# Dilated q and k as rows of eight, masks made on chip, and batch 1's attention moved to the end of gate stage 0

## The chip, the cores and the metric

The kernel runs on one NeuronCore of a Trainium2 chip. The metric is device time in microseconds for one execution. Inputs are read from and the output is written to HBM within that time.

## The reference

Eight batches of eight heads, 576 positions, head size 64. Heads 0 to 3 attend to a plain causal window of 32 positions, heads 4 to 7 to a dilated one (every fourth position, 32 of them). The attention output, 4608 tokens of 512 features, goes through a GEGLU block.

```python
mask_plain = (rel >= 0) & (rel < 32)
mask_dil = (rel >= 0) & (rel < 32 * 4) & (rel % 4 == 0)
scores = q @ k.T / 8, masked by head, softmax          # per batch and head, 576 x 576
attn = softmax(scores) @ v                             # (8, 8, 576, 64)
x = attn.transpose(0, 2, 1, 3).reshape(4608, 512)
out = (gelu(x @ w_gate) * (x @ w_val)) @ w_out         # 512 -> 1536 -> 512
```

q, k, v and the weights are float32, as is the output. The kernel computes in float16 with float32 sums.

## The kernel before

**Tiling.** The block runs in nine stages, one for each chunk of 512 tokens. A stage has 12 gate blocks (`ffn1`: for each block of 128 of the 1536 hidden features, four matmuls with `w_gate` and four with `w_val` over the four k-chunks `xT[0..3]`, then `geglu`, Gelu on ScalarE and the product on VectorE into `u_all`) and then four output blocks of 128 tokens (`ffn2`: 12 matmuls with `w_out`, then `store`). Attention is cut into 32 pairs of heads, four for each batch (`n // 4` is the batch; pairs 0 and 1 of batch 0 are plain, 2 and 3 dilated), and each pair fills 576 columns of one `xT[g]`. The attention of batch c + 1 is computed within stage c, mostly between matmuls of `ffn2`, by hooks.

**One pair of heads.** `emit_s` makes the scores in four PSUM banks from `qT` and `kT` (features on partitions), and ScalarE takes the exponential into a tile `P`. The mask comes in one of two ways: with `pe_mask` TensorE first writes a bias (0 or -60000, `bias_p` or `bias_d`) into the banks by a matmul with the identity; otherwise VectorE multiplies `P` by 0 or 1 afterwards (`emit_mask`). `emit_pv` multiplies `P` with ones (the denominators, part "den") and with v (part "num"). VectorE turns the denominators into reciprocals by two 32 x 32 block transposes (`norm_r` and `recip`, tiles `dt`, `rc`, `rb`) and multiplies the numerators (`norm_x`) into `xT`.

**Dilated layout.** Position 4i + r is element i of class r. Keys and queries of each class are 144 long; the first 128 are one block, the last 16 the rest; `last_keys` copies the last 64 keys of each class into `kTr` for the rest. `quads` reads four consecutive positions as one row of 1 KB.

**Start.** SP and ScalarE queues load q and k of batch 0 as rows of six (plain heads, `first_p`, 96 partitions) and rows of four (dilated heads, `first_d` with 128 partitions and `first_r` with the last 16), all float32. Pool's queue loads the identities and both masks from constants in HBM. 16 matmuls on ones (`warm`) run on TensorE while the loads are under way. Engines cast to float16, TensorE transposes (`t_plain`, `t_dil`, `t_rest`; the last from float32), and copies bring the transposes from PSUM into `qTp` and `qTd`. Pool issues the weights by casting DMA, `load_w(0..2)` (a third of `w_gate` and of `w_val` each), after its casts of q.

**Order.** It is written out by hand (`manual_schedule`): each engine runs its instructions in the order of the program text, and waits on semaphores. PSUM has eight banks, and each use names its banks. The four pairs of batch 0 are done before stage 0. In stage 0, the transposes for batch 1 follow gate blocks 8 (`t_dil`, `t_rest`), 9, 10 (`t_plain`) and 11 (`t_dil`, `t_rest`), and its scores, denominators and numerators stand at hooks in the four output blocks, which run one after another on banks 0 and 1. From batch 2 on, q and k are transposed by DMA.

**DMA order.** `gated` lets one DMA wait for the landing of another: the loads of batch 1's plain q and k wait for the second third of `w_val`, v of batch 1 for the second third of `w_out`, and the loads of batch 2 for the last third.

**Gate block 0 and 1.** In stages 0 and 1 they run together (`ffn1_two`), k-chunk by k-chunk over four bank pairs, so that each k-chunk is used as soon as its `xT` is there.

The functions that the diff touches:

Of the kernel before, what the change touches and what calls it, by code (L numbers as in the profile page):

```python
# [15 lines left out]
WIN = 32  # L16
DIL = 4
USCALE = 32.0


def _np_masks():
    p = np.arange(128)[:, None]

    def band(n, off=0):
        rel = np.arange(n)[None, :] + off - p
        return (rel >= 0) & (rel < WIN)

    main_p, last_p, tail_p = band(160), band(128), band(64, 64)
    main_d = band(128)

    rel = 48 + np.arange(16)[None, :] - p % 64
    rest_d = [(rel >= 0) & (rel < WIN) & (p // 64 == m) for m in range(2)]
    mp = np.concatenate([main_p, main_p, main_p, last_p, tail_p], axis=1).astype(np.float16)
    md = np.concatenate([main_d, rest_d[0], main_d, rest_d[1]], axis=1).astype(np.float16)
    return mp, md
# [3 lines left out]
def kernel(  # L39
# [19 lines left out]
    R6 = S // 6  # L59
    NCH = NT // CH  # L60
# [10 lines left out]

    mp_np, md_np = _np_masks()
    mp_dram = nc.inline_tensor(mp_np, name="mask_plain")
    md_dram = nc.inline_tensor(md_np, name="mask_dil")
    id_dram = nc.inline_tensor(np.eye(P, dtype=np.float16), name="attn_identity")
    id32_dram = nc.inline_tensor(np.eye(16, dtype=np.float32), name="identity_f32")
# [13 lines left out]
    ident32 = const.tile([16, 16], F32, tag="ident32")  # L90
# [31 lines left out]
    first_d = [x32[t][:, 0 : HK * 4 * D] for t in range(2)]  # L122
    first_r = [x32[2 + t][0:16, 0 : HK * 4 * D] for t in range(2)]

    def load_w(i):
        cs = slice(i * CH, (i + 1) * CH)
        nc.gpsimd.dma_start(out=wg_t[i], in_=moe_w_gate[:, cs].rearrange("(kc p) n -> p kc n", p=P))
        return nc.gpsimd.dma_start(
            out=wv_t[i], in_=moe_w_val[:, cs].rearrange("(kc p) n -> p kc n", p=P)
        )  # L130
# [27 lines left out]

    def rows(src, b, kb):
        n = min(P, S - kb * P)  # L160
        return n, src[b, 0:HK, kb * P : kb * P + n, :].rearrange("h p d -> p h d")
# [14 lines left out]
    def v_plain(b, sv, eng):  # L176
        for kb in range(5):
            k0 = min(kb * P, S - P)
            gated(eng.dma_start(out=sv[:, kb], in_=v[b, 0:HK, k0 : k0 + P, :].rearrange("h p d -> p h d")))
# [23 lines left out]
    def load_qk_dil(b):  # L203
# [6 lines left out]
        return qd, rd  # L210

# [76 lines left out]
    def t_dil(b, hp, qd, q0, k0, engs):  # L288

        qtd_ = tiles["qT", b][1]  # L290
        for t, c0 in ((0, q0), (1, k0)):
            for hl in range(2):
                for m in range(2):
                    nc.tensor.transpose(
                        ps16f[:, c0 + (2 * hl + m) * P : c0 + (2 * hl + m + 1) * P],
                        qd[:, t, 2 * hp + hl, 2 * m : 2 * m + 2, :].rearrange("p r d -> p (r d)"),
                        ident,
                    )
        for t, c0 in ((0, q0), (1, k0)):
            copy(  # L300
                engs[t],
                qtd_[:, t, 2 * hp : 2 * hp + 2].rearrange("p h m i -> p (h m) i")[:, :, 0:P],
                ps16f[:, c0 : c0 + 512].rearrange("p (c i) -> p c i", i=P),
            )

    def t_rest(b, hp, rd, r0):

        qtd_ = tiles["qT", b][1]
        f32 = rd[0].dtype == F32
        pv = (psf if f32 else ps16f)[:, r0 : r0 + P]  # L310
        for t in range(2):
            for hl in range(2):
                for m in range(2):
                    c0 = (4 * t + 2 * hl + m) * 16
                    h0 = (2 * hp + hl) * 4 * D + 2 * m * D
                    nc.tensor.transpose(
                        pv[:, c0 : c0 + 16], rd[t][:, h0 : h0 + P], ident32 if f32 else ident[0:16, 0:16]
                    )
        nc.vector.tensor_copy(
            qtd_[:, :, 2 * hp : 2 * hp + 2].rearrange("p t h m i -> p t (h m) i")[:, :, :, P:NCL],  # L320
            pv.rearrange("p (t c i) -> p t c i", t=2, i=16),
        )

    def emit_s(n, b0, pe_mask=False):
# [5 lines left out]
        if n == NHP:  # L330
            last_keys(b, 0, HK)
# [174 lines left out]
    def norm_r(n, b0, wide=False, flip=False):  # L506
        dt = nrm.tile([P, 18, 32], F32, tag="dt", bufs=1)
# [5 lines left out]
        nc.vector.transpose(dst, den)  # L513
        recip(n, dt)
# [77 lines left out]
    def ffn2(c, tb, bank, hooks=None):  # L592
        for fc in range(NNB):
# [26 lines left out]
    nc.gpsimd.dma_start(ident, id_dram.ap())  # L620
    nc.gpsimd.dma_start(mask_p, mp_dram.ap())
    for t, src, eng in ((0, q, nc.sync), (1, k, nc.scalar)):
        eng.dma_start(out=fh(first_d[t]), in_=quads(src, 0, HK, 0, 4 * P))
        eng.dma_start(out=fh(first_r[t]), in_=quads(src, 0, HK, 4 * P, S))
    nc.gpsimd.dma_start(ident32, id32_dram.ap())
    nc.gpsimd.dma_start(mask_d, md_dram.ap())
    sv0 = new_v(0)
    v_plain(0, sv0, nc.sync)
    first_vd = ldp.tile([P, HK * 4 * D], F32, tag="st", name="st0")
    nc.scalar.dma_start(out=fh(first_vd), in_=quads(v, 0, HK, 0, 4 * P))  # L630
    q6 = ldp.tile([R6, 2, 6, HK, D], F16, tag="qp", name="qp0")
    qd0 = ldp.tile([P, 2, HK, 4, D], F16, tag="qd", name="qd0")
# [3 lines left out]

    def r4(t):
        return fh(t).rearrange("p h (r d) -> p h r d", r=4)

    warm(16, 7)  # L640
# [6 lines left out]
    nc.vector.tensor_scalar(bias_p, mask_p, 1.0, 60000.0, ALU.subtract, ALU.mult)  # L647
    for hp in range(2):
        t_plain(0, q6, hp, 2 * hp, ("act", "dve"))
    nc.gpsimd.tensor_scalar(bias_d, mask_d, 1.0, 60000.0, ALU.subtract, ALU.mult)  # L650
    for hp in range(2):
        copy("pool", qd0[:, 0, 2 * hp : 2 * hp + 2], r4(first_d[0])[:, 2 * hp : 2 * hp + 2])
    load_v_dil_rest(0)
    load_w(0)
    v_cast(0, sv0)
    copy("pool", tiles["v", 0][1], r4(first_vd))
    w1 = load_w(1)
    load_w(2)

    def den(n, b0, wide=False):  # L660
        emit_pv(n, b0, ("den",), wide)
        norm_r(n, b0, wide)
# [4 lines left out]

    emit_s(0, 4, pe_mask=True)
    emit_s(1, 0, pe_mask=True)
    for hp, eng in ((0, "dve"), (1, "act")):  # L670
        copy(eng, qd0[:, 1, 2 * hp : 2 * hp + 2], r4(first_d[1])[:, 2 * hp : 2 * hp + 2])
    den(0, 4, wide=True)
    for hp in range(2):
        t_dil(0, hp, qd0, 4096 + 1024 * hp, 4608 + 1024 * hp, ("act", "dve"))
    for hp in range(2):
        t_rest(0, hp, first_r, P * hp)
    last_keys(0, 0, HK)
    den(1, 4, wide=True)
    emit_s(2, 0, pe_mask=True)
    num(0, 4)  # L680
    den(2, 4, wide=True)
    emit_s(3, 0, pe_mask=True)
    num(1, 4)
    den(3, 4, wide=True)
    num(2, 0)
    num(3, 2)


    gate["dma"] = w1
# [5 lines left out]
    qd1, rd1 = load_qk_dil(1)  # L695
# [16 lines left out]
    scores = {0: range(4, 8), 1: range(8, 12), 2: range(12, 17), 3: range(17, 22), 4: range(22, 27), 5: range(27, 32)}  # L712
    values_b = {1: range(8, 12), 2: range(12, 16), 3: range(17, 20), 4: range(22, 24), 5: range(27, 28)}
    values_a = {3: {4: 16}, 4: {2: 20, 6: 21}, 5: {1: 24, 4: 25, 7: 26}, 6: {1: 28, 4: 29, 7: 30, 10: 31}}
    biased = (6, 7, 9)
# [13 lines left out]
    for c in range(NCH):  # L729
# [5 lines left out]
        if c < 2:  # L735
            pairs = ((2, 3), (0, 1))
        else:
            pairs = (ends, (mm0 + 1, mm0 + 2))
# [136 lines left out]
```

The softmax here doesn't subtract the row's maximum and nothing guards it: scores larger than these inputs give would overflow.

## Time and profile before

| | us |
|---|---|
| median of 7 runs (lowest, highest) | 357.06 (356.34, 357.92) |
| the profiled execution | 357.03 |
| its span, first to last instruction | 355.2 |
| TensorE busy | 340.0 |
| VectorE, ScalarE, Pool busy | 203.5, 146.7, 79.3 |
| first matmul of stage 0 starts | 25.19 |
| first output block of stage 0 starts | 50.04 |
| first matmul of stage 1 starts | 67.98 |

The profile is of one execution. Its engines are PE (TensorE; PEld is its weight load), DVE (VectorE), ACT (ScalarE), POOL (GpSimd) and SP (SyncE, which issues DMAs). A line of the timeline has the start, the length, the engine, the source line, the operation with what it writes and reads, a count where like instructions are merged, and in brackets the idle time before it with what ended that. DMA issues show as DMA_DIRECT2D on the engine that issues them, and their data land later. The mean granted clock of TensorE is 0.995.

### The profile page before, as it was taken

Reading aid. Unit: us, or ns where it says so; the run is one execution under the profiler, and the core shown is the slowest. Engines: PE = TensorE matmul, PEld = TensorE weight load, DVE = VectorE, ACT = ScalarE, POOL = GpSimd, SP = SyncE. Lnnn points to the kernel's source line nnn. Section 1 sums busy time; section 2 is a strip of 40 time slices with the busy share of each in tenths; the row PEclk is TensorE's granted clock in tenths of the full one; section 3 lists DMA queues with packets and bytes.
Section 4 is the critical chain, followed back from the end, with each engine's and each line's share of the span. In section 5 each row is a group of like instructions: output and inputs, shape, how many; then the busy total and the mean of one; then the engine's idle time right before and its main releaser. Section 6 shows DMA issues by size and latency. Waiting matters only on the chain.

```text
span 355.2 us, 5974 instructions
## 1 busy us (share of the span) xinstructions
PE 340.0 (96%) x2330; PEld 164.1 (46%) x2330; DVE 203.5 (57%) x313; ACT 146.7 (41%) x217; POOL 79.3 (22%) x110
## 2 busy tenths in 40 slices
PE   7879999999999999999999999999999999999995
PEld 2554454444454444444544454444454444444442
DVE  3585456743486348784778765985399423303420
ACT  1733355253553355535562447236733223323320
POOL 2580334550413074063005400240000000000000
PEclk9899999999999999999999999999999999999999
DMA  8999999999899899999149952792200020020002
GB/s 189 243 195 215 219 152 200 179 162 248 178 116 194 183 174 142 235 181 135 61 135 193 128 117 89 168 165 56 89 2 0 31 89 1 2 89 30 2 30 89
DMA packets 107292, 45.31 MB, mean 128 GB/s; under 512 B 83040, under 2 KB 102496, under 8 KB 107264
## 3 DMA queue, kind: packets, MB, share of 16 engines
q1 hardware_dynamic: 84272, 31.21, 40.7%
q0 software_dynamic: 21456, 12.01, 26.6%
q10 hardware_dynamic: 1536, 1.70, 2.1%
q8 instruction: 18, 0.29, 0.4%
q14 instruction: 10, 0.08, 0.1%
HBM read 40.13 MB, written 9.44 MB: 140 GB/s over the span
## 4 chain that ended last, share of the span: by engine, by line
PE 68%; DMA 12%; DVE 12%; issue 3%; POOL 2%; ACT 1%; ACTq 0%; SPq 0%; DVEq 0%; POOLq 0%
PE ps L562 40%; PE ps L596 21%; PE ps L455 4%; DMA xT<-in_k_dram 4%; DMA st<-in_k_dram 3%; DMA wv<-in_moe_w_val_dram 3%; DMA wo<-in_moe_w_out_dram 2%; DVE dt L483 2%; DVE u_all L585 2%; DVE xT L537 2%; DVE rb L522 2%; DVE dt L513 2%; DVE P L383 2%; DVE xT L493 1%; DMA sv<-in_v_dram 1%
## 5 line engine op out<-in xcount | busy, mean ns | idle before, releaser
L585 DVE SCALAR_TENSOR_TENSOR u_all<-g,ps 128x512 f16<-128x512 f16 x108 | 72.8, 684 | 76.6 <-PE ps L562 68.1
L562 PE MATMUL ps<-xT,wg 128*128 128x512 f16 x432 | 114.0, 379 | 1.0 <-DVE xT L537 0.4
L562 PE MATMUL ps<-xT,wv 128*128 128x512 f16 x432 | 113.8, 379 | 0.7 <-ACT osb L607 0.3
L584 ACT ACTIVATE g<-ps 128x512 f16<-128x512 f32 x108 | 63.8, 597 | 121.3 <-PE ps L562 121.2
L596 PE MATMUL ps<-wo,u_all 128*128 128x512 f16 x432 | 100.3, 380 | 0.0
L562 PEld LDWEIGHTS <-wv 128*128 128x128 f16 x432 | 42.2, 98 | 53.3 <-issue 2.9
L562 PEld LDWEIGHTS <-wg 128*128 128x128 f16 x432 | 41.1, 98 | 48.6 <-issue 1.6
L596 PEld LDWEIGHTS <-u_all 128*128 128x128 f16 x432 | 39.4, 98 | 45.3 <-issue 0.6
L607 ACT ACTIVATE osb<-ps 128x512 f32<-128x512 f32 x33 | 19.7, 598 | 38.1 <-PE ps L596 37.5
L199 POOL CAST qp<-st 128x2048 f16<-128x2048 f32 x6 | 11.4, 1896 | 96.7 <-DMA sv<-in_v_dram 54.7
L513 DVE STREAM_TRANSPOSE dt<-ps 128x576 f32<-128x576 f32 x23 | 17.9, 777 | 14.7 <-PE ps L455 14.6
L522 DVE STREAM_TRANSPOSE rb<-rc 128x576 f32<-128x576 f32 (+4 forms) x34 | 25.3, 743 | 1.2
L375 ACT ACTIVATE P<-ps 128x1152 f16<-128x1152 f32 x16 | 18.1, 1131 | 17.1 <-PE ps L373 17.0
L353 ACT ACTIVATE P<-ps 128x960 f16<-128x960 f32 x16 | 15.5, 970 | 12.2 <-PE ps L343 12.1
L537 DVE TENSOR_TENSOR xT<-ps,rb 128x576 f16<-128x576 f32 x16 | 17.9, 1129 | 0.3
L609 DVE TENSOR_SCALAR osb<-ps 128x512 f32<-128x512 f32 x3 | 2.1, 692 | 27.8 <-PE ps L596 27.8
L455 PE MATMUL ps<-P,ones 128*64 128x96 f16 (+5 forms) x174 | 11.5, 244 | 4.6 <-DVE P L383 2.2
L383 DVE TENSOR_TENSOR P<-P,mask_p 128x1344 f16<-128x1344 f16 x14 | 12.7, 912 | 5.0 <-ACT P L354 5.0
L383 DVE TENSOR_TENSOR P<-P,mask_d 128x1152 f16<-128x1152 f16 x11 | 8.3, 755 | 10.2 <-ACT P L375 10.2
L455 PEld LDWEIGHTS <-ones 128*64 128x64 f16 x174 | 7.4, 108 | 14.1 <-issue 11.2
L183 POOL CAST vp<-sv 128x1024 f16<-128x1024 f32 x8 | 9.0, 1127 | 13.0 <-DMA sv<-in_v_dram 13.0
L483 DVE STREAM_TRANSPOSE dt<-ps 64x576 f32<-64x576 f32 x14 | 10.9, 781 | 0.4
(83 smaller groups left out, 242.8 us busy)
## 6 DMA issues: line engine op xcount, KB each, us to landing
out_dram<-osb SPq DMA_DIRECT2D x36, 256.0 KB, 2.0
sv<-in_v_dram SPq DMA_DIRECT2D x40, 128.0 KB, 3.7
st<-in_q_dram SPq DMA_DIRECT2D x24, 128.0 KB, 3.6
st<-in_k_dram SPq DMA_DIRECT2D x24, 128.0 KB, 3.6
qd<-in_q_dram POOLq DMA_DIRECT2D x7, 256.0 KB, 5.2
qd<-in_k_dram POOLq DMA_DIRECT2D x7, 256.0 KB, 7.1
vd<-in_v_dram POOLq DMA_DIRECT2D x7, 256.0 KB, 6.6
wg<-in_moe_w_gate_dram POOLq DMA_DIRECT2D x3, 512.0 KB, 7.2
```

Of the source, the lines that this page charges most:

```text
L375: nc.scalar.activation(pt, ps[:, b0 : b0 + 4, 0:DW], AF.Exp, bias=0.0, scale=scale)
L383: nc.vector.tensor_tensor(pt, pt, mb, ALU.mult)
L455: nc.tensor.matmul(o, lhs, rhs, start=st, stop=True, skip_group_check=True)
L483: nc.vector.transpose(dt[64 * hl : 64 * hl + 64].rearrange("p b c -> p (b c)"), both_rows(1 - hl, b0, hl))
L513: nc.vector.transpose(dst, den)
L522: nc.vector.transpose(rb[:, 0 : 32 * nb].rearrange("p (b c) -> p b c", c=32), bass.AP(tensor=rc.tensor, offset=rc.offset, ap=[rc.ap[0], [1 ...
L537: nc.vector.tensor_tensor(dst.rearrange("p (i m s) -> p i m s", m=2, s=2), num, rb.rearrange("p (s m i) -> p i m s", s=2, m=2), ALU.mult,)
L562: nc.tensor.matmul(ps[:, bank, :], w[:, kc, ns], xT[kc][:, tok], start=first, stop=end)
L584: nc.scalar.activation(g, ps[:, banks[0], :], AF.Gelu)
L585: nc.vector.scalar_tensor_tensor(u_all[:, nb, :], g, USCALE, ps[:, banks[1], :], ALU.mult, ALU.mult)
L596: nc.tensor.matmul(ps[:, bank, :], u_all[:, fc, tb * P : (tb + 1) * P], wo_t[fc // 4][:, fc % 4, :], start=(fc == 0), stop=(fc == NNB - 1),)
L607: nc.scalar.activation(osb, ps[:, bank, :], AF.Copy, bias=0.0, scale=1.0 / USCALE)
```

## The change

- **Dilated q and k of batches 0 and 1** are read as rows of eight positions (`eights`, 72 partitions, 2 KB a row) by one casting DMA each from Pool's queue (`load_eights`). `t_dil` has 16 transposes of 72 rows for a pair of heads where it had 8 of 128 rows and `t_rest` had 8 of 16 rows; `t_rest`, the float32 rows, their casts and the float32 identity are gone.
- **Masks and identity** are made by Pool with memsets and affine selects (`identity`, `mask_plain`, `mask_dil`); their constants and four DMAs are gone. `bias_p` is made by VectorE right after its first memset in program order, `bias_d` by VectorE instead of Pool.
- **Weights.** The first `load_w` waits for the last tile of v (`gate_v`) of batch 0. v follows q on SP's queue without waits, and the dilated v moves from ScalarE's queue to SP's, behind v. The plain q and k of batch 1 now wait for the last third of `w_gate`.
- **Attention of batch 0** is reordered: scores of both plain pairs, dilated transposes, both plain denominators, scores of both dilated pairs, then the rest. The plain numerators are copied by ScalarE and multiplied by Pool (`num_split`). `last_keys` is shared by VectorE and Pool. `warm` has 30 matmuls instead of 16.
- **Batch 1.** Only the plain transposes stay within the gate blocks, after 10 and 11. Scores of pair 4, both dilated transposes and `last_keys` follow gate block 11. Output blocks 0 and 1 run side by side on banks 2 and 3 in thirds of four matmuls (`third`), with scores 5, 6 and 7 and denominators between. The Gelu table is loaded at the end of the stage. Stages 1 to 3 use the mirrored banks.

```diff
+    def identity():
+        nc.gpsimd.memset(ident, 1.0)
+        for sign in (1, -1):
+            nc.gpsimd.affine_select(out=ident, in_=ident, pattern=[[sign, P]], ...)
+    def band(t, step, off):
+        for sign, base in ((1, off), (-1, WIN - 1 - off)):
+            nc.gpsimd.affine_select(out=t, in_=t, ...)
+    def mask_plain():
+        nc.gpsimd.memset(mask_p, 1.0)
+        band(mask_p[:, 0:PB].rearrange("p (r c) -> p r c", c=PW), 0, 0)
+        band(mask_p[:, PB : PB + P].rearrange("p (r c) -> p r c", r=1), 0, 0)
+        band(mask_p[:, PB + P : PH].rearrange("p (r c) -> p r c", r=1), 0, 64)
+        nc.vector.tensor_scalar(bias_p, mask_p, 1.0, 60000.0, ALU.subtract, ALU.mult)
+    def mask_dil():
+        nc.gpsimd.memset(mask_d, 1.0)
+        by_class = mask_d.rearrange("p (m i) -> p m i", m=2)
+        band(by_class[:, :, 0:P], 0, 0)
+        band(by_class[:, :, P:NCL], 64, 48)
...
     def load_w(i):
...
+        gated(both[0])
...
+    def load_eights(b):
+        q8 = ldp.tile([R8, 2, HK, 8, D], F16, tag="qd", name=f"qd{b}")
+        for t, src in ((0, q), (1, k)):
+            tiles["last"] = nc.gpsimd.dma_start(
+                out=q8[:, t].rearrange("p h r d -> p h (r d)"), in_=eights(src, b, HK, H)
+            )
...
-    def t_dil(b, hp, qd, q0, k0, engs):
+    def t_dil(b, hp, q8, b0, engs):
...
+                for r in range(4):
+                    c0 = ((hl * 2 + r % 2) * 2 + r // 2) * R8
                     nc.tensor.transpose(
+                        ps16[:, b0 + t, c0 : c0 + R8],
+                        q8[:, t, 2 * hp + hl, 2 * r : 2 * r + 2, :].rearrange("p r d -> p (r d)"),
+                        ident[0:R8, 0:R8],
                     )
...
-    def t_rest(b, hp, rd, r0):
...
     for t, src, eng in ((0, q, nc.sync), (1, k, nc.scalar)):
         eng.dma_start(out=first_p[:, t], in_=sixes(src, 0))
-    nc.gpsimd.dma_start(ident, id_dram.ap())
-    nc.gpsimd.dma_start(mask_p, mp_dram.ap())
-    for t, src, eng in ((0, q, nc.sync), (1, k, nc.scalar)):
-        eng.dma_start(out=fh(first_d[t]), in_=quads(src, 0, HK, 0, 4 * P))
-        eng.dma_start(out=fh(first_r[t]), in_=quads(src, 0, HK, 4 * P, S))
-    nc.gpsimd.dma_start(ident32, id32_dram.ap())
-    nc.gpsimd.dma_start(mask_d, md_dram.ap())
+    qd0 = load_eights(0)
     sv0 = new_v(0)
-    v_plain(0, sv0, nc.sync)
+    load_v_dil_rest(0)
+    identity()
+    mask_plain()
+    mask_dil()
+    gate_v = v_plain(0, sv0, nc.sync)
...
-    nc.scalar.dma_start(out=fh(first_vd), in_=quads(v, 0, HK, 0, 4 * P))
+    nc.sync.dma_start(out=fh(first_vd), in_=quads(v, 0, HK, 0, 4 * P))
...
-    warm(16, 7)
+    warm(30, 7)
...
+    gate["dma"] = gate_v
     load_w(0)
     v_cast(0, sv0)
...
+    def num_split(n, b0):
+        emit_pv(n, b0, ("num",))
+        rb = tiles.pop(("rb", n))
+        nc.scalar.copy(first_n[n], psf[:, b0 * 512 : b0 * 512 + S])
+        nc.gpsimd.tensor_tensor(xT[n][:, 0:S], first_n[n], rb, ALU.mult)
...
     emit_s(0, 4, pe_mask=True)
     emit_s(1, 0, pe_mask=True)
...
+    t_dil(0, 0, qd0, 4, ("dve", "dve"))
+    t_dil(0, 1, qd0, 6, ("act", "act"))
+    last_keys(0, 0, 2)
+    last_keys(0, 2, HK, nc.gpsimd)
+    load_w(1)
+    copy("pool", tiles["v", 0][1], r4(first_vd))
+    wg2, _ = load_w(2)
+    dt0, dt1 = (den(n, -2 * n, t.rearrange("p (b c) -> p b c", c=32)) for n, t in enumerate(first_t))
+    recip(0, dt0)
+    recip(1, dt1)
+    emit_s(2, 4, pe_mask=True)
+    emit_s(3, 0, pe_mask=True)
+    den(2, 4)
+    num_split(0, 4)
+    num_split(1, 0)
+    emit_pv(2, 2, ("num",))
+    den(3, 4)
+    norm_x(2, 2)
+    num(3, 0)
...
-    gate["dma"] = w1
+    gate["dma"] = wg2
...
-    qd1, rd1 = load_qk_dil(1)
+    qd1 = load_eights(1)
...
+            s_of(4)
+            t_dil(1, 0, qd1, 2, ("dve", "dve"))
+            t_dil(1, 1, qd1, 0, ("dve", "dve"))
+            last_keys(1, 0, HK)
+            mask_next()
+            third(0)
+            s_of(5)
+            den(4, -2)
+            third(1)
+            mask_next()
+            s_of(6)
+            den(5, -2)
+            third(2)
+            s_of(7)
+            ffn2(c, 2, 2, {3: [lambda: den(6, -2)], 9: [lambda: num(4, 4)]})
+            store(c, 2, 2, "act")
+            ffn2(c, 3, 3, {0: [lambda: den(7, -2)], 4: [lambda: num(5, 6)]})
+            store(c, 3, 3, "act")
+            num(6, 0)
+            num(7, 4)
+            gelu_table()
```

## The prediction

> **What bounds the kernel now.** I read the page first, then the table of stages, then the timelines of TensorE and Pool at the start, then VectorE at the end of stage 0.
>
> ```profile
> PE 340.0 (96%) x2330; PEld 164.1 (46%) x2330; DVE 203.5 (57%) x313; ACT 146.7 (41%) x217; POOL 79.3 (22%) x110
> ...
> PE 68%; DMA 12%; DVE 12%; issue 3%; POOL 2%; ACT 1%; ACTq 0%; SPq 0%; DVEq 0%; POOLq 0%
> ```
>
> TensorE is the bound nearly everywhere, and of the chain only the 12% on DMA and 12% on VectorE can be had back. The table of stages (columns: span, then busy time and count for each engine, granted clock, DMA share, GB/s) says where:
>
> ```profile
> 8.00:25.20 17.20, 12.80 (x181) 8.68 (x181) 12.57 (x23) 10.15 (x14) 11.52 (x16) 0.90 1.22 223
> 25.20:29.70 4.50, 3.97 (x21) 1.57 (x18) 3.50 (x5) 0.78 (x2) 2.27 (x4) 1.00 1.24 206
> 29.70:49.20 19.50, 19.27 (x121) 9.53 (x120) 9.61 (x16) 7.86 (x14) 6.61 (x9) 1.00 1.08 194
> 49.20:68.00 18.80, 17.97 (x182) 8.95 (x181) 12.93 (x22) 8.53 (x12) 6.83 (x8) 1.00 1.17 196
> ```
>
> The change touches these 68 us alone. The wide matmuls come 0.216 us apart (four in 0.86), so what counts is when they begin, and how much else stands between them. TensorE at the first gate stage:
>
> ```profile
> 25.73 0.39 PE L562 MATMUL ps<-xT,wv 128*128 128x512 f16 x1
> ...
> 27.79 0.38 PE L562 MATMUL ps<-xT,wg 128*128 128x512 f16 x1 [0.37 <-DVE xT L537]
> ...
> 29.68 1.03 PE L562 MATMUL ps<-xT,wg 128*128 128x512 f16 x4
> ```
>
> The first value matmul waits for `wv` (landed 25.72), the third and fourth k-chunks for VectorE's normalisation. The opening 16 matmuls end at 29.68; I call that moment E. From E to stage 1 (67.98) it takes 38.30 us. Pool:
>
> ```profile
> 2.98 0.59 POOL L626 DMA_DIRECT2D mask_d<-mask_dil  x1
> 10.82 1.19 POOL L650 TENSOR_SCALAR bias_d<-mask_d 128x288 f16<-128x288 f16 x1 [7.26 <-DMA mask_d<-mask_dil]
> 13.59 1.18 POOL L264 CAST qd<-xT 128x512 f16<-128x512 f32 x2 [1.58 <-DMA xT<-in_q_dram]
> ...
> 16.79 0.77 POOL L128 DMA_DIRECT2D wv<-in_moe_w_val_dram  x1
> ```
>
> Pool idles from 3.57 to 10.82. In the built program a library reload for Pool stands just before that TENSOR_SCALAR; it has no row, and whatever it costs lies in this gap. After the change the same reload stands before the first affine select, with nothing to hide it.
>
> **Masks on chip.** Four mask and identity DMAs go. Pool gets 3 memsets and 12 affine selects; identity and `mask_p` take 8 selects over 1600 columns, `mask_d` 4 over 576. No row is an affine select. Nearest: Pool casts (512, 1024, 2048 columns: 0.62, 1.04, 1.90 us), so 0.19 us plus 0.83 ns a column. Memsets at that rate make 1.05 us, the 8 selects 8 x 0.19 + 1600 x 0.83 ns = 2.85: 3.9 us. The other end is the TENSOR_SCALAR above, 4.1 ns a column: 7.6 us. I take 3.9, since 1.19 us for 288 columns looks like a first call. Pool first issues four DMAs (0.77, 0.77, 0.65, 0.65 from 1.22): free at 4.1. `mask_p` is ready at M = 8.0 without a reload cost, 11.7 with slow selects, and 15.2 if the reload costs all of the 7.2 us gap (its bounds are 0 and 7.2; I take 0, as the gap ends with the landing of `mask_d`, which explains it alone). A gain from the operation itself is excluded: it only adds to Pool.
>
> The Trainium skill speaks against this step: its page "GPSIMD Engine Reference", section 2.1 "Instruction dispatch", says that the first call after a code load pays some 6 us that no profile row shows. No row here shows that cost or excludes it; with it M would be 14.0, and an estimate by my sum would end near 360.
>
> Who waits: VectorE. `bias_p` is its second instruction, ahead of the memsets and the casts of q (1.03 us), so these wait for M + 0.34. Transposes end at M + 1.9 (casts 1.03, last 12 transposes 0.52). On the other side the 30 warm-up matmuls: 16 took 6.47 us at 0.427 apart, the change of rate showing near 7.1 us; 14 more at 0.216 end at 10.9, and 24 transposes at 43 ns make 11.95. So M is covered up to 10.0; beyond that each us counts. In return TensorE stays warm: the clock stood at 0.50 from 12 to 14 us, and the mask matmuls took 1.32 us where the dilated ones later take 0.65.
>
> **Eights by cast DMA.** Casts of `qd0` (Pool 1.18, VectorE 0.89, ScalarE 0.62) and 16 f32 remainder transposes (2 x 0.67 us, with a 0.73 us wait) go. In bytes landed, 3.9 MB ahead of the weights become 3.1, as dilated q and k land in f16 and the masks go. Up to v it is 2.6 MB: from 2 us at the 223 GB/s of the second stretch 13.5. q8 and k8 stand before half of v, so they are in time for their transposes at 14.6. v has 256-byte rows; 12 to 14 us, when they ran, had 154 GB/s, so I take v at 15 to 16.5. vd moves to SP's queue behind v, and is needed at 21.
>
> **w gated by v.** Pool issues w0 when the last v tile lands. The same transfer from an empty queue is in the trace: `wo` 1 and 2, issued from 44.04 (DMA share 0.33), landed by 52.49, 8.45 us. So w0 is there at 23.5 to 25, where it was 25.7. Behind the gated issue on Pool stand the v casts (1.50 us), half of `last_keys`, w1, the vd cast, w2 and two multiplies; `last_keys` is wanted first, for scores 3 at 18.5, and done at about 18.6.
>
> **Attention of batch 0.** From 11.95: scores 0 (0.65 + 0.40), exps to 14.6 and 16.1 (1.45 each), dilated transposes and copies to 17.3, first `dt` at 16.6. From there VectorE is unbroken: four `dt` at 0.78, four reciprocal pairs at 1.07, two products at 1.1 = 9.6 us, so the last xT at 26.2, and its four matmuls end at 27.1. The products of pairs 0 and 1 leave VectorE: ScalarE copies the numerators (0.64 each) after the last exp, 20.8 to 22.1, and Pool multiplies (no such row; between a 576-column cast, 0.67, and twice VectorE's 0.73; I take 1.0) after issuing w2 at 22.6, so 23.6 and 24.6. With w0 at 23.5 to 25 the 16 matmuls (3.46) end at 27.1 to 28.5. I take E = 27.6, which is 2.1 earlier.
>
> **Rest of stage 0.** Of E to the end of gate block 11 (19.54 us), one pair of dilated transposes (1.23) and one plain set (0.51) leave. From there to stage 1 were 18.76, of which 1.0 stalls:
>
> ```profile
> 58.02 1.68 DVE L383 TENSOR_TENSOR P<-P,mask_p 128x1344 f16<-128x1344 f16 x1
> 60.26 0.78 DVE L513 STREAM_TRANSPOSE dt<-ps 128x576 f32<-128x576 f32 x1 [0.57 <-PE ps L455]
> ```
>
> (the late mask, 0.79 on TensorE, and 0.2 for `wo`). The new order: 18.76 - 1.0 - 0.82 (old dilated set) + 0.51 + 2 x 0.69 (16 transposes at 43 ns) = 18.83, plus new waits. Scores 4 need banks 6 and 7, still held by the last plain transposes: 0.75. `den` 4 waits for its mask behind four copies on VectorE (0.42 or 0.75 each by the two copy rows; I take 0.75), `kTr` 0.29 and the mask 0.86: 1.3. `den` 5: 0.25. Sum 21.1; with 17.8 before it 38.9 against 38.3: +0.6. The Gelu table, now loaded ahead, spares the 0.3 stall at 73.2: +0.3. With the stalls at 0.8 or 3.3 instead it is -1.2 to +1.3. The rows of batch 1 wait for wg2 where it was wv1, but with 0.8 MB less ahead they land by about 40 (41.67 before); w1, w2 and `wo` are issued at about the same time or earlier. Later stages mirror their banks: nothing.
>
> **Sum.** -2.1 + 0.3 = -1.8. The profiled execution took 357.03 us (span 355.2), the median of the runs is 357.06. Forecast 355.2. What this kernel's measurement can tell from no change is about 0.2%, or 0.7 us.
>
> **The rivals.**
> 1. *Slower: Pool is late with the masks.* For it: the reload that has no cover any more, and VectorE standing behind it. Against: a gap that the mask's landing explains. It decides from M = 11.9, where the 1.8 us are used up: a reload of 3.9 us with fast selects. At 7.2 us, M = 15.2, 5.2 late, and TensorE idle after the warm-up, so again half clock (about 1 us): E = 33.8, and the end +4.4: 361.4.
> 2. *The gate costs what it saves.* v's small rows share DMA with q8 and k8. At 17.5 for v, w0 is there at 25.95, E = 29.4 and the end at 357.1; if v lands at 18.67, as it did, 358.2. Against: its tiles are now all issued by 4 us, where SP used to wait for the rows of q and k until 14.2.
> 3. *No change: slow selects alone*, M = 11.7, 1.7 late: 356.9.
>
> **How the numbers follow.** Forecast case 0.52 (own range 353.3 to 356.2, the tail's ends with E at 27.1 or 27.6); rival 1 0.27, rival 2 0.11 (0.04 of it within the bound), rival 3 0.10. Faster by over 0.2%: 0.52; within: 0.14; slower: 0.34. The range goes from 353.3 (E = 27.1, tail -1.2) to 361.0, close to the full reload.
>
> **What would show it.** Right: Pool's last select of `mask_p` before 10, `bias_p` at once, transposes at 10.9, clock 1.00 from 11 to 14; E at 27 to 28.5; gate block 11 to stage 1 about 21 us with waits of `den` 4 on its mask. Wrong: a gap on Pool before the first select; casts of q after 11; a wait for `wv` beyond 25; waits of TensorE on `qd` or `wo` in stage 0.

## The result, and the profile after

The changed kernel takes 356.04 us (median of 19 runs, 355.25 to 356.88), the kernel before 357.55 (47 runs beside them). The ratio is 0.9957, 95% interval 0.9947 to 0.9967: faster by about 1.5 us, where 1.8 were forecast. (The forecast of 355.2 was counted from 357.06; from the 357.55 measured here it would be 355.75.) The profiled execution of the changed kernel took 355.55 us with a span of 353.8 (before: 357.03 and 355.2). One execution of the run e9 below, the profiled one, ran at a granted clock of 0.56 throughout and took 579.77 us; no median and no ratio below has it in.

The number came out; the sum behind it only in part, and most of this document is about that. First the table of stages of the changed kernel (columns as before: stretch, its length, busy time and count of PE, PEld, DVE, ACT, POOL, granted clock, DMA share, GB/s). The stretches end at the first gate matmul, at E (the end of the opening 16 gate matmuls), at the end of gate block 11 and at the start of stage 1:

```profile
8.00:23.99 15.99, 11.83 (x192) 8.07 (x191) 13.49 (x28) 11.13 (x15) 10.41 (x18) 1.00 1.09 181
23.99:27.93 3.94, 3.61 (x16) 1.54 (x16) 1.93 (x2) 0.45 (x1) 3.52 (x4) 1.00 1.25 207
27.93:46.87 18.94, 17.96 (x94) 8.36 (x93) 8.24 (x12) 7.25 (x13) 3.70 (x5) 1.00 0.93 179
46.87:67.43 20.56, 19.11 (x210) 10.17 (x208) 14.72 (x24) 9.25 (x12) 6.77 (x11) 1.00 1.11 181
```

E is at 27.93 instead of 29.68: 1.75 us gained. From E to stage 1 it takes 39.50 instead of 38.30: 1.20 lost. Stage 1 starts 0.55 earlier. It opens without the stall behind the table load, and the last store leaves VectorE at 350.82 instead of 351.61: 0.79 earlier. The other 0.6 us of the span lie behind that moment: about 3.0 us from there to the end of the span instead of 3.6. The last copy of a store, before and after:

```profile
350.92 0.69 DVE L609 TENSOR_SCALAR osb<-ps 128x512 f32<-128x512 f32 x1 [9.60 <-PE ps L596]
```

```profile
350.13 0.69 DVE L622 TENSOR_SCALAR osb<-ps 128x512 f32<-128x512 f32 x1 [9.60 <-PE ps L609]
```

TensorE in stage 0 of the changed kernel:

```profile
23.99 0.38 PE L575 MATMUL ps<-xT,wg 128*128 128x512 f16 x1 [1.64 <-POOL xT L676]
...
25.34 0.38 PE L575 MATMUL ps<-xT,wg 128*128 128x512 f16 x1 [0.33 <-POOL xT L676]
...
44.87 0.43 PE L305 MATMUL ps<-ident,qp 96*128 96x96 f16 x6 [0.98 <-POOL qp L292]
...
53.17 0.48 PE L463 MATMUL ps<-P,ones 128*64 128x512 f16 x6 [0.81 <-DVE P L391]
```

In what follows w0, w1 and w2 are the three thirds of the weights, each with a gate half (`wg`) and a value half (`wv`), and the rows of batch 1 are its plain q and k (`st`). The first gate matmul waits for Pool's product; the weights were there, but not by much (`wv` of w0 landed 7.7 us after its issue at 16.07, at about 23.8). At gate block 10 the transposes of batch 1 wait 0.98 us for Pool's cast of rows that have only just landed. The chain of waits (start, length, what) shows that both waits hang on Pool's queue:

```profile
5.40 9.61 DMA sv<-in_v_dram
...
16.83 1.08 POOL vp L203
...
20.03 0.98 POOL vd L292
21.01 11.30 DMA wg<-in_moe_w_gate_dram
...
32.74 11.20 DMA st<-in_k_dram
...
45.30 1.74 PE ps L575 x8
```

From the landing of v the chain goes down Pool's queue to the issue of w2, through w2's landing to the issue of batch 1's rows, and through their landing to TensorE at gate block 10. E is not on it.

### The profile page after: what moved, and what is told of

Read it like the earlier page. It is cut to its first block, busy times and chain, and to the rows that moved or that the text cites. A ratio compares the mean times of both kernels' runs of the same rounds, so it can differ in the third digit from the quotient of the medians.

```text
span 353.8 us, 5997 instructions
## 1 busy us (share of the span) xinstructions
PE 338.4 (96%) x2338; PEld 163.7 (46%) x2338; DVE 201.4 (57%) x307; ACT 147.8 (42%) x219; POOL 81.4 (23%) x121
## 4 chain that ended last, share of the span: by engine, by line
PE 71%; DVE 12%; DMA 9%; issue 3%; POOL 2%; SPq 1%; ACT 1%; DVEq 0%; POOLq 0%; ACTq 0%
PE ps L575 41%; PE ps L609 22%; PE ps L463 4%; DMA wg<-in_moe_w_gate_dram 3%; DMA st<-in_k_dram 3%; DMA sv<-in_v_dram 3%; DVE u_all L598 2%; DVE dt L491 2%; DVE xT L550 1%; DVE xT L501 1%; PE ps L381 1%; DVE rb L535 1%; DVE P L391 1%; DVE dt L524 1%; SPq L197 1%
## 5 line engine op out<-in xcount | busy, mean ns | idle before, releaser
L524 DVE STREAM_TRANSPOSE dt<-ps 128x576 f32<-128x576 f32 x21 | 16.3, 777 | 15.1 <-PE ps L463 15.1
L391 DVE TENSOR_TENSOR P<-P,mask_p 128x1344 f16<-128x1344 f16 x14 | 11.9, 856 | 2.6 <-ACT P L362 2.5
L491 DVE STREAM_TRANSPOSE dt<-ps 64x576 f32<-64x576 f32 x14 | 10.9, 781 | 0.4
```

The costliest lines, as they stand in the source:

```text
L391: nc.vector.tensor_tensor(pt, pt, mb, ALU.mult)
L491: nc.vector.transpose(dt[64 * hl : 64 * hl + 64].rearrange("p b c -> p (b c)"), both_rows(1 - hl, b0, hl))
```

## The experiments

All were timed beside the kernel before; times below are medians, to be held against 356.04 for the changed kernel, and the ratios are to the kernel before. The kernel before had medians of 357.13 to 357.59 beside them, so that runs of different rounds are compared more surely by their ratios. The theory after the reading above was: E is set by Pool's queue, counted from the landing of v, and the tail's loss by the release of batch 1's rows through w2. The rival: weights, VectorE or the masks' chain set E.

### e1_w2_late

```diff
-    load_w(1)
+    _, wv1 = load_w(1)
     copy("pool", tiles["v", 0][1], r4(first_vd))
-    wg2, _ = load_w(2)
...
     num_split(1, 0)
+    load_w(2)
...
-    gate["dma"] = wg2
+    gate["dma"] = wv1
```

> The third weight chunk (w2) is issued by Pool behind its two multiplies instead of ahead of them, and the rows of batch 1 are released by the second chunk's value half instead of w2's gate half. Theory: the moment E (end of the opening 16 gate matmuls, 27.93 in the changed kernel) is set by Pool's queue, counted from the landing of v. Then the multiplies start when ScalarE's copies are done (21.2 and 21.9), the first gate matmul comes at 22.6 to 23.2 and E falls to 26.8 to 27.3, where VectorE's last product (25.9) sets it; the 1.0 us wait for Pool's casts of batch 1 goes too. Together 1.2 to 2.0 us less than the changed kernel: 354.0 to 354.9. Rival: the first weights themselves set E (TensorE's weight load also stood waiting for wv until 23.99), then E stays at 27.7 to 27.9 and only the second part shows, 355.0; and w2, issued 3 us later, would show as a wait at gate block 8.

Measured: 354.75, ratio 0.9927 (0.9913 to 0.9942), 1.3 us less than the changed kernel. Pool's products start at 21.41 instead of 22.50, the first gate matmul comes at 22.87, and E at 27.12: the theory's place. What sets E now is not VectorE's last product, as the theory had it, but the first weights, as the rival had it, with a wait of 0.63 us for `wv`:

```profile
21.41 2.76 POOL L676 TENSOR_TENSOR xT<-xT,rb 128x576 f16<-128x576 f32 x2 [0.16 <-ACT xT L675]
...
23.87 0.39 PE L575 MATMUL ps<-xT,wv 128*128 128x512 f16 x1 [0.63 <-DMA wv<-in_moe_w_val_dram]
```

The wait at gate block 10 did not go: it is 0.86. The rows' last half was issued 2.3 us earlier than in the changed kernel (30.43), but took 12.6 us instead of 11.2, so that Pool's cast of it starts at 43.06, only 0.93 earlier. w2, issued at 24.13, was under way beside it; that the sharing is the cause is argued, not shown. The gain of 0.9 at stage 1 (66.56 instead of 67.43) is the rows' gain as much as E's.

### e2_st_w1

```diff
-    gate["dma"] = wg2
+    gate["dma"] = wv1
```

> Only the release of the rows of batch 1: the second chunk's value half instead of w2's gate half. Theory: of the 1.2 us by which E to stage 1 grew (38.30 to 39.50), 1.0 is TensorE's wait for Pool's cast of those rows at 44.87; they are issued at 32.74 because wg2 releases them. Released some 3 us earlier they land by 41, the wait goes, and the time falls by 0.8 to 1.0 us: 355.0 to 355.3. Rival: the DMA engines are full (1.1 busy share and more) and the rows share them with w2, so they land as late as before, or w2 lands late instead: no change, 356.0, or a wait at gate block 8.

Measured: 355.50, ratio 0.9940 (0.9917 to 0.9963). The cast of the late half starts at 41.99 instead of 43.99 and the wait is gone:

```profile
41.99 2.37 POOL L292 CAST qp<-st 96x768 f16<-96x768 f32 x3 [3.91 <-DMA st<-in_k_dram]
```

But the seven executions fall in two groups: three with a mean granted clock of 1.00 at 354.26 to 354.42, four with 0.993 to 0.995 at 355.50 to 356.20. The profiled one is of the second kind. Its stretches from 20 us on:

```profile
20.00:24.00 4.00, 1.93 (x48) 1.52 (x45) 3.86 (x8) 3.25 (x4) 4.00 (x5) 0.97 1.23 205
24.00:26.00 2.00, 1.86 (x5) 0.71 (x5) 2.00 (x3) 0.00 (x0) 2.00 (x3) 0.50 1.24 206
26.00:28.00 2.00, 2.00 (x8) 0.75 (x6) 0.09 (x1) 0.00 (x0) 1.66 (x3) 0.70 1.24 207
```

TensorE was busy for 1.93 of the 4 us before 24, with 1.62 idle at the end, and then ran at half clock for about 3 us: the first gate matmuls are 0.43 apart instead of 0.216, and E is 29.09. So the theory's 0.8 to 1.0 was too small where the clock held (1.7), and in the others, if they ran as the profiled one did, the half clock ate nearly all of it.

### e4_masks_dma

```diff
+    nc.gpsimd.dma_start(ident, id_dram.ap())
+    nc.gpsimd.dma_start(mask_p, mp_dram.ap())
     qd0 = load_eights(0)
...
-    identity()
-    mask_plain()
-    mask_dil()
+    nc.gpsimd.dma_start(mask_d, md_dram.ap())
+    nc.vector.tensor_scalar(bias_p, mask_p, 1.0, 60000.0, ALU.subtract, ALU.mult)
```

> The masks and the identity by DMA from inline tensors again, as in the kernel before; all else as in the changed kernel. Theory: the start is bound by the bytes ahead of v; 0.35 MB of masks at the 223 GB/s of the stretch from 8 to 24 us are 1.6 us, so v lands at 16.6 instead of 15.0, w0 and Pool's queue move with it, and E comes 1.0 to 1.6 us later: 357.0 to 357.6. Rival: v does not move, as the DMA engines have room, and the masks come sooner than from Pool (bias_p before 8.3, casts of q with it): no change or up to 0.5 us faster, 355.5 to 356.0.

Measured: 357.96, ratio 1.0014 (0.9998 to 1.0029): without masks on chip the rest of the change gains nothing against the kernel before. By the medians the step is worth 1.9 us, but only 1.5 of it lies within the span (its last store leaves VectorE at 352.31 instead of 350.82). The rest lies outside it: in each of the twelve executions the time is 2.2 us longer than the span, in the changed kernel 1.7. Why, no run tells. Two Pool lines and one of VectorE:

```profile
16.24 0.76 POOL L162 DMA_DIRECT2D wg<-in_moe_w_gate_dram  x1 [10.42 <-DMA sv<-in_v_dram]
...
19.71 0.40 POOL L281 COPY kTr<-qTd 128x256 f16<-128x256 f16 x1 [0.59 <-ACT qTd L312]
```

```profile
9.55 0.34 DVE L661 TENSOR_SCALAR bias_p<-mask_p 128x672 f16<-128x672 f16 x1 [8.15 <-DMA mask_p<-mask_plain]
```

v is there 0.94 later (16.24 instead of 15.30), less than the 1.6 of the expectation, which took 0.35 MB for masks that are 0.27 in the profile of before (and 223 GB/s, which is the rate of the kernel before). And the mask by DMA is later than Pool's own: `bias_p` starts at 9.55 instead of 8.31, the transposes at 12.39 instead of 11.26, the clock falls to 0.63 from 12 to 16 us, and `kTr` on Pool then waits for this chain, not for v. E is 29.53; the k half's wait ends at 46.35 instead of 44.87.

### e5_ones_late

```diff
-    for vp_, _, vt_, _ in vset:
-        ...
     for hp in range(2):
         for t in range(2):
             cast_six(("dve", "act")[t], q6, first_p, t, hp)
     for hp in range(2):
         t_plain(0, q6, hp, 2 * hp, ("act", "dve"))
+    for vp_, _, vt_, _ in vset:
+        ...
     nc.vector.tensor_scalar(bias_d, mask_d, ...)
```

> VectorE's six memsets of ones in the value tiles (1.9 us, which stood between bias_p and the casts of q) move behind the transposes' copies. Theory: E is set through Pool by the landing of v (15.0), not by the masks' chain: the transposes come 0.8 to 1.0 us earlier (10.3 instead of 11.26), scores, exps and the dt of pairs 0 and 1 with them, but E stays within 0.3 of 27.93 and the time within 0.3 of 356.0. Rival: the chain masks, casts, transposes, scores, exps, dt, products sets E; then E and the time fall by 0.8 to 1.0, to 355.1.

Measured: 355.98, ratio 0.9963 (0.9949 to 0.9976): no change, as the theory said, with the transposes at 10.02 instead of 11.26 and the first denominators on TensorE at 14.86 instead of 16.10. With the gate on v, this chain has slack. E itself is 30.08 in the profiled execution, not within 0.3 of 27.93: behind an idle 1.84 us thirteen of the sixteen opening matmuls ran at half clock, 0.43 apart. Yet stage 1 starts only 1.0 later than in the changed kernel (68.42), since TensorE then no longer waits at gate block 10. The profiled execution, at 356.50, is one of three with a clock of 0.989 or 0.990, which took 356.50 to 356.64; the other six took 355.47 to 356.11.

### e10_fill

```diff
     num(3, 0)
+    warm(7, 4)
```

> Seven warm-up matmuls more (1.5 us at 0.216 apart, into a bank that the first gate block overwrites) in the 1.64 us in which TensorE waits for Pool's first product; nothing else changes. Theory: after such an idle stretch the granted clock falls to 0.50 in some executions (in the runs so far the opening 16 matmuls came 0.43 apart behind waits of 1.62 and 1.84 us), which moves E by 1 to 2 us; but in the changed kernel E does not set the time as long as it lies before about 29, because TensorE then waits at 44.87 for Pool's cast of the rows of batch 1, which are released by wg2. So the mean granted clock of all executions is 0.998 or more, and the time stays within 0.3 of 356.0. Rival: E sets the time, and the changed kernel's executions at 0.993 to 0.995 pay for the clock: then 355.3.

Measured: 355.86, ratio 0.9953 (0.9937 to 0.9970), all eight executions at a clock of 0.998 or more. Of the changed kernel's 20 executions (the profiled one included) 13 had a clock of 0.993 to 0.995, and they took no longer (median 356.04, the others 355.95). So the changed kernel has half clock in most executions and its time shows nothing of it. E itself can be seen in the profiled ones alone (28.02 here); that it came later in the 13 is inferred from their clock. What sets the time is the landing of the rows of batch 1, for which TensorE waits here too:

```profile
45.04 0.43 PE L305 MATMUL ps<-ident,qp 96*128 96x96 f16 x6 [1.06 <-POOL qp L292]
```

### e3_no_gate

```diff
-    gate["dma"] = gate_v
     load_w(0)
```

> The first weights are no longer held back until the last tile of v has landed: Pool issues them at about 10 us; all else as in the changed kernel. Theory: 1.05 MB of weights (f16 as landed; 5 us at the 205 GB/s of the following stretch) share the DMA engines with v, so v lands 2 to 4 us after 15.0; Pool's casts and products move by that less the 1.5 us of the two issues, E comes 1 to 2.5 us later, of which 1.0 is covered by the wait for the rows of batch 1: 356.0 to 357.8. Rival: w0 sets E, v hardly moves: the same or up to 0.5 us faster, 355.5 to 356.0.

Measured: 354.17, ratio 0.9906 (0.9886 to 0.9927), 1.9 us less than the changed kernel. The theory, that v would pay, was wrong by sign; the rival had the sign and v, but a quarter of the size, and its reason (w0 sets E) is not the one that the trace shows. Pool's queue in the ungated kernel:

```profile
9.88 0.78 POOL L140 DMA_DIRECT2D wg<-in_moe_w_gate_dram  x1
10.65 0.82 POOL L140 DMA_DIRECT2D wv<-in_moe_w_val_dram  x1
15.13 1.04 POOL L203 CAST vp<-sv 128x1024 f16<-128x1024 f32 x1 [3.65 <-DMA sv<-in_v_dram]
...
17.31 0.40 POOL L259 COPY kTr<-qTd 128x256 f16<-128x256 f16 x1 [0.81 <-ACT qTd L290]
...
41.66 2.37 POOL L292 CAST qp<-st 96x768 f16<-96x768 f32 x3 [2.44 <-DMA st<-in_k_dram]
```

The last tile of v is there by 15.13 although the weights were issued at 9.88; in the gated kernel Pool's wait for it ended at 15.30. Holding the weights back bought v nothing. What it cost is in the DMA view from 14 to 18 us, 40 slices of 0.1 us, first the gated kernel, then the ungated one:

```profile
DMA  9999876656655552810000000009900002399986
```

```profile
DMA  9999999999999999999999999999999999999999
```

From 15.8 the engines have, but for one short burst, nothing to do until the weights that were issued at 15.30 begin to arrive at about 17.3 (112 GB/s from 16 to 20 us; 209 in the ungated kernel). Besides, their two issues (1.5 us) stand behind the landing of v on Pool in the gated kernel. Without the gate E is 27.07, and it is Pool's queue that brings this: the products start at 21.65 instead of 22.50. `wg` of w2 is issued 0.84 earlier and lands 9.3 us after that instead of 11.3, so the rows' late half is cast at 41.66 instead of 43.99, without a wait, and stage 1 starts at 65.41 instead of 67.43. No run separates the shorter queue on Pool from the DMA engines' idle time.

### e6_selects_twice

```diff
         nc.gpsimd.memset(mask_p, 1.0)
+        for _ in range(2):
+            band(...)   # the three bands of mask_p, twice
```

> The six selects of mask_p are done twice, which changes nothing in the mask and makes it ready 2.39 us later (M = 10.66 instead of 8.27). Theory: transposes at about 13.6 instead of 11.26, scores, exps, dt and VectorE's products 2.4 later (last product 28.3), Pool's products less; E about 29.2; of these 1.25 us 1.0 is covered by the wait for the rows of batch 1: plus 0.2 to 0.6 us, 356.2 to 356.7. Rival one, the rule of the forecast (M is covered up to 10.0 and each us beyond counts): plus 0.7, 356.7. Rival two: the whole delay passes through, 358.4.

Measured: 357.32, ratio 0.9995 (0.9982 to 1.0007): plus 1.3 us for 2.39 of delay, between the rule of the forecast and the full price. TensorE ran dry after the warm-up (2.58 us), the clock fell to 0.77 from 12 to 16 us, and `kTr` on Pool waited 2.40 for ScalarE, with w1, the vd cast, w2 and the products behind it:

```profile
20.89 0.40 POOL L260 COPY kTr<-qTd 128x256 f16<-128x256 f16 x1 [2.40 <-ACT qTd L291]
```

E is 30.60, all of the delay and a little more. Some 1.0 of it is covered by the 0.98 that the changed kernel waits at gate block 10 anyway; that wait is gone here. The theory had VectorE delayed and had left Pool out.

### e7_before_table

```diff
             num(7, 4)
+            gelu_table()
```

> The kernel before, with one line more: the Gelu table is loaded at the end of stage 0. Theory: the stall at the start of stage 1 (0.3 us at 73.2, behind the table load) goes, nothing else moves: 0.3 us less than the kernel before, 357.2. Rival: ScalarE is still behind for another reason (its stores), or TensorE regains the stall later: no change, 357.5.

Measured: 357.27 against 357.59 for the kernel before, ratio 0.9990 (0.9977 to 1.0003). The point is the expected 0.3; the interval holds none as well, so it is not settled by this run. The two traces of stage 1 agree with it: in the kernel before a gap of 0.30 stands before 73.47, and in this one none.

### e8_old_tail

To the ungated kernel, the stage 0 of before is put back for batch 1 (rows of four, transposes in gate blocks 8 to 11, the old order in FFN2), and its rows are released by `wv1`:

```diff
-    qd1 = load_eights(1)
+    qd1, rd1 = load_qk_dil(1)
...
-            if c == 0 and nb > 9:
-                t_plain(1, q61, nb - 10, 4 + 2 * (nb - 10), ("act", "dve"))
+            if c == 0 and nb in (9, 10):
+                t_plain(1, q61, nb - 9, 4 + 2 * (nb - 9), ("act", "dve"))
+            if c == 0 and nb in (8, 11):
+                ...
```

> The ungated kernel (w at about 10 us, run before this at 354.17) with the attention of batch 1 as in the kernel before: q and k of its dilated heads as rows of four with 32 small transposes for the remainders, transposed in gate blocks 8 to 11, its scores, denominators and numerators inside the FFN2 of stage 0 in the old order, the masks of pairs 4 and 5 on VectorE, no Gelu table at the end of stage 0; the rows of batch 1 are released by the second weight chunk's value half. Theory: the new order of stage 0 brings nothing by itself (E to stage 1 took 38.30 before and 38.34 in the ungated kernel); with the old one E stays at 27.1 and stage 1 starts 38.3 to 38.8 later, the excess being a wait for Pool's cast, since the old order wants the rows of batch 1 1.7 us earlier; the table load costs 0.3 again: 354.3 to 355.0. Rival: the new order saves the 1.0 us of stalls that the old one had (the late mask and wo), so the old one is 1.3 or more slower: 355.5 or more.

Measured: 353.63, ratio 0.9897 (0.9880 to 0.9913), against 0.9906 for the ungated kernel with the new order: within the intervals the same, so nothing shows that the new order brings anything. The earlier release of the rows does not blur this, as the ungated kernel had no wait for them. By the traces E to stage 1 is 37.72 with the old order and 38.34 with the new; the old one then pays 0.44 behind the table load:

```profile
70.56 0.81 PE L612 MATMUL ps<-xT,wg 128*128 128x512 f16 x3 [0.44 <-ACT g L634]
```

### e9_free_ones and e13_free_all

e9 is the ungated kernel with the edit of e5; e13 adds that of e1.

```diff
-    gate["dma"] = gate_v
     load_w(0)
...
     (the six memsets behind t_plain, as in e5)
...
-    wg2, _ = load_w(2)
...
     num_split(1, 0)
+    load_w(2)
...
-    gate["dma"] = wg2
+    gate["dma"] = wv1
```

(The lines from `wg2` on are e13's alone.)

> Ungated, and VectorE's six memsets of ones behind the copies of the transposes. Theory: with v's gate gone from Pool's queue, what sets E is the chain masks, casts of q, transposes, copies (Pool waited 0.81 at 17.31 for ScalarE's copies of the dilated rows), so here, unlike with the gate, the memsets' 1.0 us on that chain comes back: E 26.1 to 26.4 instead of 27.07; of that 0.2 to 0.5 may go into a wait for the cast of the rows of batch 1 at gate block 10. Time 353.3 to 353.8 against 354.17. Rival: VectorE or the weights set E, and it stays at 27.0: 354.2.

> The same with the third weight chunk issued behind Pool's two products and the rows of batch 1 released by the second chunk's value half. Theory: Pool's products start as soon as ScalarE's copies are there (about 19.9), so VectorE's last product (24.8 to 25.0) sets E, 25.9 to 26.2, and the rows of batch 1, released 1 to 2 us earlier, are in time: 352.6 to 353.4. Rival: the bytes in the DMA queues set the landing of rows and weights from here on (the engines are busy throughout from 8 to 32 us), so that the wait moves to gate block 4, 8 or 10, and the time stays at the e9 kernel's.

Measured: e9 352.98 (four executions), ratio 0.9878 (0.9859 to 0.9897). The memsets that cost nothing behind the gate cost about 1 us without it, as the theory said, though the intervals of the two ratios (0.9906 for the ungated kernel) still touch, and where E lies in e9 no trace shows. e13: 352.73, ratio 0.9873 (0.9855 to 0.9891), E 26.40 (25.9 to 26.2 expected), the rows' late half cast at 41.10 without a wait. The time is inside the theory's range; against e9 it is 0.2 less, which the intervals do not separate.

### e14_best

The kernel of e8 with two edits more:

```diff
     (the six memsets behind t_plain, as in e5)
...
             num(7, 4)
+            gelu_table()
```

> Ungated, ones late, the old order of stage 0 (run before this at 353.63) and the Gelu table at its end; the third weight chunk stays ahead of Pool's products. Theory: what was gained at the start and what was gained by the old order add up: E 26.3 to 26.5 from the ones, 37.7 from E to stage 1 as in the old order's run, no stall of 0.44 behind the table load: 0.6 plus 0.4 less than 353.63, 352.4 to 352.9, about as the e13 kernel (352.73). Rival: with an earlier E the old order waits for wo (0.55 already at 49.95 in its run) and for Pool's cast of the rows of batch 1, so that the start's gain is lost: 353.3 to 353.6.

Measured: 352.37, ratio 0.9859 (0.9842 to 0.9876): the fastest version, some 3.5 us below the changed kernel by the ratios. E is 26.16, E to stage 1 37.59, no stall behind the table; the rival's wait for `wo` is there with 0.43. It is the changed kernel with w ungated, ones late, and the old stage 0 of batch 1 (order, rows of four, release by `wv1`). e13 has the same release and the table load too, and takes 38.40 from E to stage 1: by these two traces the new stage 0 of batch 1 takes 0.8 us longer than the old one, where e8 and the ungated kernel differ by 0.6 before the 0.44 of the table. The times, 352.73 and 352.37, do not show it by themselves, as their intervals overlap.

## Why the prediction was right, and where it was not

**Masks on chip.** M was 8.27 where 8.0 was forecast, `bias_p` followed at 8.31, the casts of q 0.95 us from 10.71 and the transposes at 11.26 (10.9 forecast). The sum left out VectorE's memsets of ones, 1.9 us. In the kernel before they ran at the start, while VectorE had nothing else to do; the change puts `bias_p`, which waits for Pool, ahead of them. The first of them before, and the lines around them after:

```profile
1.46 0.48 DVE L642 MEMSET vp<- 128x512 f16 x1
```

```profile
8.31 0.44 DVE L128 TENSOR_SCALAR bias_p<-mask_p 128x672 f16<-128x672 f16 x1 [6.83 <-POOL mask_p L113]
8.80 0.48 DVE L648 MEMSET vp<- 128x512 f16 x1
...
10.71 0.95 DVE L294 CAST qp<-u_all 96x768 f16<-96x768 f32 x2
```

```profile
11.26 1.19 PE L305 MATMUL ps<-ident,qp 96*128 96x96 f16 x24 [1.03 <-DVE qp L294]
```

The warm-up was over at 10.23 and did not cover this: TensorE stood idle for 1.03 us. That it cost nothing is luck: the sum looked for the cover in the warm-up, and it came from the landing of v, for which Pool's queue waited anyway (e5). The reload cost nothing that can be seen: Pool is done with the memset of `ident` at 4.48, and the first select starts at 4.55.

```profile
4.55 0.66 POOL L106 TENSOR_SCALAR_AFFINE_SELECT ident<-ident 128x128 f16<-128x128 f16 x2
5.16 0.66 POOL L124 MEMSET mask_p<- 128x672 f16 x1
5.88 2.39 POOL L113 TENSOR_SCALAR_AFFINE_SELECT mask_p<-mask_p 128x480 f16<-128x480 f16 x6
```

Rival 1 fell with it. The 6 us that the Trainium skill's "GPSIMD Engine Reference", section 2.1, gives for a first call after a code load are not in this trace. What the prediction did not do is give the step a value by itself: it costed it at nothing and left the gain in the start. By e4 it is 1.5 us within the span, with fewer bytes ahead of v and an earlier `bias_p`; the two are not separated. That M is covered up to 10.0 was too generous: e6 at M = 10.60 cost 1.3 us, where the rule gives 0.6. What the rows of eight and the new order of batch 0's attention bring by themselves no run tells.

**v and the gate.** v landed at 15.0 by the chain (Pool's wait for it ended at 15.30), inside the 15 to 16.5. That the gate is a gain was the wrong step, and the one that mattered: the prediction argued from w0's 8.45 us from an empty queue, and never asked what v would lose without the gate. By e3 v loses nothing and the gate costs 1.9 us. Rival 2 had the sign (the gate does not earn its cost) by another way: v late, which it was not.

**E.** Measured 27.93, forecast 27.6. The forecast let w0 set it (23.5 to 25, and 3.46 for the 16 matmuls). w0 came as forecast, at about 23.8, and VectorE was on time (last product done at 25.91, forecast 26.2), but Pool set E: its products took 1.43 us each, not 1.0, so the first matmul started at 23.99 and the fifth had to wait another 0.33. The number is close because two paths end within 0.2 us of each other. In most executions E was probably later than that, because of the half clock behind such an idle stretch (e2, e5), which the prediction did not have: it had looked at the clock from 11 to 14 us alone.

**Rest of stage 0.** Here the sum failed by a term: "The rows of batch 1 wait for wg2 where it was wv1, but with 0.8 MB less ahead they land by about 40" was costed at nothing. The late half was cast from 43.99, 0.98 of wait. wg2 landed 11.30 us after its issue. The 0.98 is four fifths of the difference between 39.50 and 38.30. The rest of the sum was too long: `den` 4 waited 0.81 (1.3 forecast) and scores 4 0.46 in two waits (0.75 forecast), and without the wait for the rows E to stage 1 takes 38.34 (e3), where 38.9 was forecast. So two errors stand against each other in the 39.50: 1.2 for the rows, and 0.6 the other way. As the rows' landing hangs on Pool's queue and not on E, a gain at E alone could not get past it: e10 shows it, and e2 that 1.7 us come back with an earlier release when the clock holds.

**Table and end.** TensorE stands 0.85 earlier behind the place of the old table stall, as with the 0.3 forecast, and 0.79 at the last store. So by the prediction's own steps the kernel gained 0.8 us; that the number came out is luck, by 0.6 us at the end of the span that the prediction did not have. The traces show where these lie. At the end of the program SP waits for the semaphores of the DMA queues one after another (L870 before, L897 after):

```profile
SPq L870 <- DMA out_dram<-osb: 1.5, 1, 1.5
SPq L870 <- PEq L870: 1.0, 2, 0.8
```

```profile
SPq L897 <- DMA out_dram<-osb: 1.2, 1, 1.2
SPq L897 <- PEq L897: 0.7, 2, 0.5
```

The last store takes 2.0 us from issue to landing in both. In the kernel before five more such waits of 0.06 us stand behind that landing, in the changed kernel one: 0.24 us. Another 0.30 lies between Pool's last two instructions, 0.38 us apart before and 0.08 after. The ten profiles of experiments on the changed kernel other than e9's (with e8's and e14's old tail and e4's masks by DMA among them) have about 3.0 us there, the two with the start of before (before and e7) 3.6. Which edit of the start does that no run tells; it stays open, but neither the masks nor the new order of stage 0 is needed for it.

## What to carry to other kernels

A transfer that is held back until another has landed is a cost to be priced like any other: look at whether the first one gains by it, and how long the DMA engines stand idle between the landing and the first bytes of what was held. Before a moment like E is credited to the end, follow the chain of waits from it: if a later transfer is released along another way, its landing is a floor, and a gain ahead of it is worth only what the floor lets through. The same edit (memsets out of a chain) can be worth nothing and 1 us, by what stands beside it, so small edits are worth trying again after each larger one. And an instruction that will wait should not stand ahead of work that could run meanwhile: here `bias_p` pushed 1.9 us of memsets into the chain.

## What the runs showed of the hardware

TensorE lost its full clock after quite short idling. In the profiled execution of e2, with 1.93 of 4 us busy and an idle 1.62 at the end, it then ran at a granted clock of 0.50 for about 3 us, and the mean clocks of three more of the seven executions (0.993 and 0.994) fit the same. The profiled execution of the changed kernel, with 1.77 of 4 us busy and an idle 1.64, kept a clock of 1.00. With seven more matmuls in such a gap (e10) the mean clock was 0.998 or more in all eight executions. The Trainium skill's "TensorE: Matmul & The Clock Gate", Part 1, speaks of an idle window of about 3.4 us that runs freely; the varying outcome from one execution to the next agrees with a free-running window, but here 1.6 us of complete idleness, in a half-idle stretch, were enough.

Weights issued by Pool's queue on nearly idle DMA engines delivered hardly anything for some 2 us: issued from 15.30, first steady data at about 17.3.
